# Attention features and a feed-forward layer on one core: the low bits of the converted weights move off POOL, and the scheduler's constants are new

## The chip, the cores and the metric

The kernel runs on one core of one Trainium2 chip. The metric is device time in microseconds (us) of one execution; lower is better. The result is compared with the median of the runs of the kernel before.

## The reference

Attention is computed with random positive features, and its output goes through a feed-forward layer. Inputs: q, k, v of 8 batches x 8 heads x 576 tokens x 64, omega 128 x 64, w_in 512 x 2048, w_out 2048 x 512.

```python
def phi(x):                                  # x scaled by 64 ** -0.25
    proj = np.einsum('bhsd,md->bhsm', x, omega)
    h = proj - np.sum(x * x, axis=-1, keepdims=True) / 2.0
    h = h - np.max(h, axis=-1, keepdims=True)
    return np.exp(h) / np.sqrt(m)
q_p, k_p = phi(q_s), phi(k_s)
kv = np.einsum('bhsm,bhsd->bhmd', k_p, v)
z = np.sum(k_p, axis=2)
num = np.einsum('bhsm,bhmd->bhsd', q_p, kv)
den = np.einsum('bhsm,bhm->bhs', q_p, z)[..., None] + 1e-06
x = (num / den)            # to 4608 tokens x 512
h = x @ w_in
out = np.maximum(0.01 * h, h) @ w_out
```

The two weight matrices arrive as 64-bit floating-point numbers, and the kernel reads them as pairs of 32-bit words.

## The kernel before

The 4608 tokens are cut into 9 blocks of 512. For each block a query stage computes the attention output x of 4 head pairs, and a feed-forward stage multiplies x by w_in, applies the leaky maximum and multiplies by w_out. While the feed-forward of block j runs, the attention of block j+1 is prepared. Large products are made of fp16 pieces: a 32-bit value is split into a high fp16 part and a low one (the rest), and three products of parts are summed. The helper `high` makes a high part or a scaled copy (L446/L448 on DVE or L450 on ACT), `low_` makes a low part by subtraction (L456, on POOL or DVE), and `two` adds or subtracts two tiles (L1048, on POOL or DVE). From block 3 on, the first product goes by a seven-product scheme whose mixed weights pass through a scratch in DRAM (`w1s`). The last two blocks use it for the second product too.

Before the first feed-forward stage the weights have to be made ready. `Weight.load` brings each matrix in 8 pieces of 1 MB into one of 4 `big` buffers (tiles fix_big). `Weight.convert` turns one piece of 128 x 1024 64-bit numbers into 32-bit ones in three steps: ACT scales the high words (L570), POOL takes the top three bits of the low words into a temporary (L573), and DVE shifts the former and joins the latter in (L575). PE then sums squares of the result (L582). From the largest sum (L590 on DVE, a PE broadcast at L484, five short DVE instructions) comes one power of two for the matrix, `pow_w`, and `Weight.split` makes the two fp16 parts with it (L448, L450, L456, L601).

The first query block and the first two key batches are computed in 32 bits (`Whole`): a load of qT or kT, squares on ACT (L733), products on PE (L759), a maximum and a subtraction on DVE (L766, L787), exponentials on ACT (L790, L979), the key sums on PE (L880), which are copied out as `kv` (L448/L450 to fix_kv), and the query's products with them (L1006). A division (L1016 to L1019, DVE) gives x in the tiles fix_x and fix_y. `turned_parts` splits x (L450 on ACT, L456 on POOL or DVE, tiles fix_xn) and turns it by a DMA transpose (L933, tile fix_xt). The first feed-forward products (L1374) read fix_xt.

The order of the work isn't written by hand. `Plan` collects some 3100 operations with the engines that may run each, a cost in us for each, and priorities. `Plan.order` then plays a list schedule: it takes the open operations by priority, gives each the engine that is free first by its rules (`PRICE` weighs an engine, `ONLY` forces one), and fixes each engine's order. `TURNS` shifts the priority of single operations, `HELD` delays single ones, `LATER` and `PACE` set priorities of whole stages (weights, keys, queries), and `S_GATE` says after which feed-forward operation the mixed weights may start. Each engine then runs its instructions strictly in that order, as does the queue of SP, which issues every DMA. Where the schedule leaves PE without work for 0.4 us or more, `between` lays filler matmuls that nobody reads (`busy`, L1447).

## Time and profile before

| | |
|---|---|
| median of 3 runs | 935.9 us (931.59 to 936.74) |
| the profiled execution | 934.14 us, of it the span from first to last instruction 932.4 us |
| PE busy | 901.2 us (97%), 8543 matmuls |
| DVE / ACT / POOL busy | 748.3 (80%) / 550.8 (59%) / 384.4 us (41%) |
| mean granted TensorE clock | 0.988 of full speed |
| HBM traffic over the span | 105 GB/s; all DMA 157 GB/s |

The profile shows one execution. PE is TensorE's matmuls and PEld its weight loads, DVE is VectorE, ACT is ScalarE, POOL is GpSimd, and SPq is the queue of SyncE. A busy PE counts pipelined matmuls, so 97% doesn't say that it works at its peak all the time. "idle before" a group is the time in which its engine waited for it, with the one that released it.

### The profile page before, as it was taken

The numbers are of one execution on the slowest core, as the hardware profiler recorded it, in microseconds if no ns is written. First come the engines' busy times: TensorE is split into PE (matmuls) and PEld (weight loads), VectorE is DVE, ScalarE is ACT, GpSimd is POOL, SyncE is SP. The second block draws the span as 40 slices with busy tenths as digits, with TensorE's granted clock in tenths as the row PEclk, the third lists the DMA queues.
The fourth block names the chain that finished last, engine by engine and source line by source line (L and its number), as shares of the span: only waits on it lengthen the run. The fifth ranks groups of instructions, "written<-read, shape, count | busy, mean of one in ns | idle before, by whom it ended". The sixth has DMA issues, their size and how long they took to land.

```text
span 932.4 us, 21056 instructions
## 1 busy us (share of the span) xinstructions
PE 901.2 (97%) x8543; PEld 617.5 (66%) x8543; DVE 748.3 (80%) x1355; ACT 550.8 (59%) x899; POOL 384.4 (41%) x311
## 2 busy tenths in 40 slices
PE   7789999999999998999999999989999999999997
PEld 7687555555545444588558855776568646888886
DVE  5689777799989987888888798968868885785872
ACT  5557776647634554568657686668558633552640
POOL 5957733334313542214222441214135556541550
PEclk9989999999999999999999999999999999999999
DMA  8867336963566549796886969597739962532401
GB/s 351 329 190 226 69 72 158 207 173 73 114 157 170 138 131 206 174 210 193 160 186 164 218 145 219 126 197 148 162 78 245 185 114 65 174 80 70 136 1 46
DMA packets 258769, 145.92 MB, mean 157 GB/s; under 512 B 191344, under 2 KB 238704, under 8 KB 257648
## 3 DMA queue, kind: packets, MB, share of 16 engines
q1 hardware_dynamic: 258672, 144.58, 64.0%
q8 instruction: 67, 1.10, 0.5%
q14 instruction: 30, 0.25, 0.1%
HBM read 81.36 MB, written 16.78 MB: 105 GB/s over the span
## 4 chain that ended last, share of the span: by engine, by line
PE 74%; DMA 10%; DVE 8%; POOL 5%; issue 2%; ACT 1%; SPq 1%; DVEq 0%; ACTq 0%; POOLq 0%
PE fixps_ffn L1396 24%; PE fixps_ffn L1282 16%; PE fixps_ffn L1374 10%; PE lateps_ffn L1282 5%; PE lateps_ffn L1206 5%; PE attps_pj L680 4%; POOL fix_wt L573 4%; PE fixps_ffn L1206 3%; DMA proj_t<-proj_z 2%; DMA fix_xt<-fix_xn 2%; DMA w1s<-fix_y 2%; DMA att_qp<-att_ph 1%; PE attps_mi L999 1%; DVE proj_st L687 1%; DMA fix_big<-w_in 1%
## 5 line engine op out<-in xcount | busy, mean ns | idle before, releaser
L1396 PE MATMUL fixps_ffn<-fix_wt,fix_big 128*128 128x512 f16 x1344 | 304.2, 381 | 0.0
L1396 PEld LDWEIGHTS <-fix_big 128*128 128x128 f16 x1344 | 127.2, 98 | 145.6 <-issue 2.2
L1282 PEld LDWEIGHTS <-fix_wt 128*128 128x128 f16 x2016 | 195.3, 98 | 25.9 <-issue 0.7
L1282 PE MATMUL fixps_ffn<-fix_xt,fix_wt 128*128 128x256 f16 x1572 | 182.5, 274 | 0.5 <-ACT fix_row L450 0.5
L456 POOL TENSOR_TENSOR fix_big<-fix_row,fix_big 128x512 f16<-128x512 f32 x66 | 85.3, 1293 | 154.7 <-ACT fix_big L450 124.1
L1374 PE MATMUL fixps_ffn<-fix_xt,fix_wt 128*128 128x512 f16 x576 | 129.2, 379 | 1.2 <-DMA fix_xt<-fix_xn 1.2
L1374 PEld LDWEIGHTS <-fix_wt 128*128 128x128 f16 x576 | 54.9, 98 | 64.4 <-issue 1.5
L687 DVE TENSOR_REDUCE proj_st<-attps_pj 128x8 f32<-128x1024 f32 x68 | 72.6, 1074 | 13.8 <-PE attps_pj L680 13.6
L709 ACT ACTIVATE att_p<-att_p,shift 128x1024 f32<-128x1024 f32 x52 | 59.4, 1143 | 32.5 <-DVE att_p L706 32.3
L450 ACT ACTIVATE fix_big<-fix_row 128x512 f16<-128x512 f32 x115 | 70.1, 624 | 11.8 <-DVE fix_row L1048 7.1
L573 POOL TENSOR_SCALAR fix_wt<-fix_big 128x1024 uint32<-128x1024 uint32 x16 | 65.1, 4070 | 13.5 <-DMA fix_big<-w_in 11.0
L456 DVE TENSOR_TENSOR fix_big<-fix_row,fix_big 128x512 f16<-128x512 f32 x73 | 62.6, 868 | 5.9 <-ACT fix_big L450 5.3
L706 DVE SCALAR_TENSOR_TENSOR att_p<-attps_pj,proj_sc,proj_st 128x1024 f32<-128x1024 f32 x52 | 66.2, 1276 | 0.1
L456 DVE TENSOR_TENSOR att_ph<-att_p,att_ph 128x1024 f16<-128x1024 f32 x48 | 62.2, 1296 | 4.5 <-ACT att_ph L450 4.5
L640 ACT ACTIVATE proj_z<-proj_nat 128x512 f32<-128x512 f32 (+1 forms) x56 | 36.3, 648 | 49.5 <-DMA proj_t<-proj_z 30.5
L456 POOL TENSOR_TENSOR fix_xn<-fix_x,fix_xn 128x512 f16<-128x512 f32 (+1 forms) x23 | 26.5, 1154 | 87.6 <-ACT fix_xn L450 75.9
L1305 ACT ACTIVATE fix_row<-fix_row 128x512 f32<-128x512 f32 x69 | 42.8, 624 | 19.1 <-DVE fix_row L1297 18.7
L680 PE MATMUL attps_pj<-om,proj_t 64*128 64x128 f16 x1416 | 50.5, 217 | 2.7 <-DMA proj_t<-proj_z 2.7
L450 ACT ACTIVATE att_ph<-att_p 128x1024 f16<-128x1024 f32 x49 | 51.5, 1050 | 2.1 <-PE attps_mi L894 1.6
L1282 PE MATMUL lateps_ffn<-fix_xt,fix_wt 128*128 128x256 f16 x444 | 51.4, 273 | 0.0
L680 PEld LDWEIGHTS <-proj_t 64*128 64x128 f16 x1416 | 39.7, 94 | 17.7 <-issue 10.8
L664 DVE SCALAR_TENSOR_TENSOR proj_z<-proj_nat,proj_sc,proj_z 128x512 f16<-128x512 f32 (+1 forms) x52 | 47.0, 906 | 4.1 <-ACT proj_z L450 3.9
(237 smaller groups left out, 1729.1 us busy)
## 6 DMA issues: line engine op xcount, KB each, us to landing
fix_wt<-w1s SPq DMA_DIRECT2D x38, 512.0 KB, 4.7
fix_wt<-w1s SPq DMA_DIRECT2D x38, 384.0 KB, 3.6
fix_v<-vn SPq DMA_DIRECT2D x16, 650.0 KB, 5.7
out<-fix_row SPq DMA_DIRECT2D x34, 256.0 KB, 2.3
...
```

The costliest lines, as they stand in the source:

```text
L450: ("ACT", act(n, int(pointer)), lambda: nc.scalar.activation(dst(), src(), AF.Copy, scale=1.0 if scale is None else value()), False),
L456: o = ways([(e, c, lambda g=g: g.tensor_tensor(dst(), a(), b(), op=ALU.subtract), True) for e, c, g in (("POOL", pool_(n), nc.gpsimd), ("D ...
L573: ways([("POOL", pool_(1024), lambda: nc.gpsimd.tensor_scalar(top3(), low(), 2.0 ** -29, 7.0, op0=ALU.mult, op1=ALU.min), True)], r=[b], w ...
L664: op("DVE", stt(n) + 0.15, lambda: nc.vector.scalar_tensor_tensor(zl(), heads(), up(), zh(), op0=ALU.mult, op1=ALU.subtract), port=True, r ...
L680: nc.tensor.matmul(at(pj)[:, 512 * h + c * M:512 * h + (c + 1) * M], at(self.t)[r, 2 * (c0 + c) + x, :], om[r, w, :], start=(x + w == 0), ...
L687: op("DVE", dve(n * M), lambda: nc.vector.tensor_reduce(row(0), pv(), axis=AX.X, op=ALU.max), r=[pj], w=[st], prio=prio)
L706: op("DVE", dve(n * M), lambda: nc.vector.scalar_tensor_tensor(p(), pv(), down(), row(2).rearrange("p (g o) -> p g o", o=1).broadcast_to([ ...
L709: op("ACT", act(n * M, 1), lambda: nc.scalar.activation(flat(p()), flat(p()), AF.Exp, bias=shift), w=[p32], r=["ones"], prio=prio)
L1206: nc.tensor.matmul(o, ga(gp, f, 1)[:, 0, P * t:P * t + P], w(f, wp), start=(first and place + f % 2 + t + gp + wp == 0), stop=(place == 3 ...
L1282: nc.tensor.matmul(o, unit(at(wb[c]), u)[:, wp, P * a:P * a + P], mixes[j, c][n][1](xp), start=(first and a == 0 and i == 0), stop=(a == 1 ...
L1374: nc.tensor.matmul(at(ph), wk[wp][:, c:c + P], xt[:, xp, :], start=(k + wp + xp == 0), stop=(k == KT - 1 and wp == 1))
L1396: nc.tensor.matmul(at(po), part(f, gp)[:, t * P:(t + 1) * P], wf[wp], start=(n == 0 and f % 4 == 0 and gp == wp), stop=(n == 3 and f % 4 = ...
```

## The change

One edit changes what is computed where. The top three bits of a low word are no longer made on POOL (a multiply and a minimum on 32-bit integers). They are made either on ACT, which reads the upper 16 bits of the low word, multiplies by 7.49 / 65536 and rounds to an integer, or on DVE, which shifts the low word right by 29. The scheduler picks: of the 16 pieces, 11 go to ACT (4 of w_in, 7 of w_out) and 5 to DVE (4 and 1). The ACT way rounds where the others cut off.

The other edits are numbers of the scheduler: the cost of the square sums 0.5 to 0.6, of a group of exponentials by 0.04 less, the cost of the 32-bit products, and all tables and weights.

```diff
+U16 = mybir.dt.uint16
-PACE = {'k': 20.5, 'q': 15.5, 'w1': 23, 'w1s': 0, 'w2': 8, 'w2s': 2}
+PACE = {'k': 11.5, 'q': 31.5, 'w1': 26, 'w1s': 4, 'w2': 12, 'w2s': 0}
-LATER = {'s': 40.0, 'w1': -245.0, 'w2': -440.0, 'k': -700.0, 'q': -375.0, 'm': 1860.0}
+LATER = {'s': 330.0, 'w1': -260.0, 'w2': -555.0, 'k': -190.0, 'q': -1135.0, 'm': 1985.0}
-S_GATE = 24
+S_GATE = 18
-PJ, PJ32 = 0.07, 0.5
+PJ, PJ32 = 0.07, 0.53
+LOW3 = 7.49 * 2.0 ** -16
 TURNS = {
-    4: -7005.2331, 7: -5110.3778, 15: -57900.145, 21: -5388.6643, 30: -5105.2668, 37: 5334.3764, 42: -2222.8973,
+    4: -5217.9625, 15: -29625.3333, 30: -29636.835, 64: 775.2483, 69: 5964.4575, 70: 8369.6977, 71: 2070.5909,
...
 ONLY = {
-    38: "DVE", 91: "DVE", 174: "DVE", 176: "DVE", 180: "DVE", 181: "POOL", 184: "POOL", 242: "POOL", 246: "DVE",
+    92: "ACT", 94: "POOL", 128: "DVE", 129: "DVE", 133: "DVE", 138: "DVE", 143: "DVE", 158: "DVE", 178: "POOL",
...
-    PRICE = {'PE': 1.0, 'ACT': 2.464, 'DVE': 7.416, 'POOL': 4.818, 'SP': 1.0}
+    PRICE = {'PE': 1.0, 'ACT': 2.957, 'DVE': 6.674, 'POOL': 2.341, 'SP': 1.0}
...
-            ways([("POOL", pool_(1024), lambda: nc.gpsimd.tensor_scalar(top3(), low(), 2.0 ** -29, 7.0, op0=ALU.mult,
-                   op1=ALU.min), True)], r=[b], w=[tmp], prio=prio)
+            ways([("ACT", act(1150), lambda: nc.scalar.activation(top3(), at(b).bitcast(
+                   U16).rearrange("p (a b) -> p a b", b=4)[:, :, 1], AF.Copy, scale=LOW3), False),
+                  ("DVE", 0.85, lambda: nc.vector.tensor_scalar(top3(), low(), 29, None, op0=ALU.logical_shift_right), True)],
+                 r=[b], w=[tmp], prio=prio)
...
-            op("PE", 0.5, squares, r=[f], w=[self.sums], prio=prio, slack=6.0)
+            op("PE", 0.6, squares, r=[f], w=[self.sums], prio=prio, slack=6.0)
...
-                op("ACT", n * (act(M, 2) - 0.07), powers, r=[pj, st, self.sc], w=[p32], prio=prio)
+                op("ACT", n * (act(M, 2) - 0.11), powers, r=[pj, st, self.sc], w=[p32], prio=prio)
```

The operations are the same in number, but nearly all stand elsewhere in the order of their engine. Lines of the changed file lie 5 higher up to the conversion and 7 higher behind it (L456 is L461 there, L933 is L940). Three places show the move. The names are those of tiles: fix_xn is the split x of a head pair, fix_wt a piece of a weight, fix_big a loaded piece, fix_kv the copied key sums, att_qp the query's exponentials, fix_row_92 here a piece of qT or its square.

POOL, first part of the program; before, from its fifth piece of the weights on:

```order
L837 COPY row_scale<-pow_v_130 128x1 x4
L837 COPY row_scale<-pow_v_130 64x1
L573 TENSOR_SCALAR fix_wt_73<-fix_big_88 128x1024
L573 TENSOR_SCALAR fix_wt_75<-fix_big_89 128x1024
L573 TENSOR_SCALAR fix_wt_77<-fix_big_90 128x1024
L573 TENSOR_SCALAR fix_wt_79<-fix_big_91 128x1024
L456 TENSOR_TENSOR fix_xn_86<-fix_x_84,fix_xn_86 128x512
L456 TENSOR_TENSOR fix_wt_67<-fix_wt_68,fix_wt_67 128x1024
```

and now, from its first computing instruction on:

```order
L844 COPY row_scale<-pow_v_130 128x1 x4
L844 COPY row_scale<-pow_v_130 64x1
L461 ISA
L461 TENSOR_TENSOR fix_xn_86<-fix_x_84,fix_xn_86 128x512
L461 TENSOR_TENSOR fix_wt_67<-fix_wt_68,fix_wt_67 128x1024
L461 TENSOR_TENSOR fix_wt_65<-fix_wt_66,fix_wt_65 128x1024
L461 TENSOR_TENSOR fix_xn_87<-fix_y_85,fix_xn_87 128x512
```

The low part of the first head pair's x stood behind 8 conversions on POOL and stands behind none.

SP's queue around the first transpose; before:

```order
L558 DMA fix_big_90<-w_out 128x2x1024
L732 DMA proj_nat_177<-kT 128x512
L558 DMA fix_big_91<-w_out 128x2x1024
L933 DMA_TRANSPOSE fix_xt_99<-fix_xn_86 128x8x128
L732 DMA fix_row_92<-qT 128x512
L732 DMA proj_nat_178<-kT 128x512
```

and now:

```order
L563 DMA fix_big_90<-w_out 128x2x1024
L940 DMA_TRANSPOSE fix_xt_99<-fix_xn_86 128x8x128
L563 DMA fix_big_91<-w_out 128x2x1024
L739 DMA proj_nat_177<-kT 128x512
L739 DMA fix_row_92<-qT 128x512
L739 DMA proj_nat_178<-kT 128x512
```

The load of qT for the fourth head pair stands behind that transpose in both.

DVE where the second pair of key sums is copied out; before:

```order
L446 CAST fix_wt_67<-fix_wt_68 128x1024
L456 TENSOR_TENSOR fix_wt_65<-fix_wt_66,fix_wt_65 128x1024
L601 SCALAR_TENSOR_TENSOR fix_wt_80<-fix_wt_64,pow_w_132,fix_wt_80 128x1024
L448 TENSOR_SCALAR fix_kv_81<-attps_mi_173,pow_v_130 128x4x64
L1016 TENSOR_SCALAR att_r_165<-fixps_ffn_115 128x4
L1017 RECIPROCAL att_r_165<-att_r_165 128x4
L766 TENSOR_REDUCE proj_st_189<-attps_pj_171 128x8
```

and now ACT, which has taken the copy:

```order
L455 ACTIVATE fix_wt_66<-fix_wt_66,pow_w_132 128x1024
L740 ACTIVATE proj_z_180<-proj_nat_178 128x512
L455 ACTIVATE fix_kv_81<-attps_mi_173,pow_v_130 128x4x64
L455 ACTIVATE fix_wt_65<-fix_wt_66 128x1024
L455 ACTIVATE fix_kv_81<-attps_mi_173 128x4
L986 ACTIVATE att_qp_163<-fixps_ffn_115,shift 128x512
```

The copy stood behind two parts of w_in on DVE, and stands behind one scaled copy of w_in and a square on ACT.

Counted over the program: POOL's two-input instructions (L456 and L1048 before) go from 243 to 291, those of DVE on the same lines from 259 to 210. DVE gets 22 more casts, 4 more copies and 9 more scaled copies (L446 and L448), besides its 5 shifts. The filler matmuls go from 113 to 70, those ahead of the first L1374 from 104 to 57. PE's other matmuls are the same in number, ahead of the first L1374 and behind it.

## Rows read from the trace of the kernel before

**Rows 1.** Stretches: PE, PEld, DVE, ACT, POOL busy (instructions), granted clock, DMA share, GB/s

```profile
25.00:50.00 25.00, 20.66 (x227) 18.35 (x229) 17.35 (x29) 12.42 (x17) 24.54 (x11) 0.86 0.89 323
50.00:75.00 25.00, 22.10 (x233) 21.05 (x232) 21.93 (x34) 16.87 (x22) 14.02 (x6) 0.86 0.45 133
90.00:150.00 60.00, 59.41 (x484) 32.73 (x484) 45.95 (x89) 45.25 (x81) 35.21 (x26) 1.00 0.36 84
150.00:350.00 200.00, 198.31 (x1618) 102.62 (x1617) 177.25 (x329) 107.26 (x178) 76.20 (x64) 1.00 0.64 150
350.00:600.00 250.00, 246.37 (x2621) 164.83 (x2620) 215.48 (x433) 167.26 (x275) 75.40 (x80) 0.99 0.82 179
```

**Rows 2.** Waits of PE from 95 us on: us in total, times, longest

```profile
PE attps_mi L1001 <- DMA att_qp<-att_ph: 3.2, 2, 3.0
PE attps_pj L680 <- DMA proj_t<-proj_z: 2.7, 5, 1.6
PE attps_mi L999 <- DVE fix_y L1019: 2.6, 1, 2.6
```

**Rows 3.** The chain that ended last, 48 to 92 us: start, us, what

```profile
47.86 2.20 POOL fix_xn L456
...
51.48 5.51 DMA fix_row<-qT
...
60.31 3.12 DVE fix_wt L456
63.43 3.06 DVE fix_wt L601
66.49 0.40 DVE fix_kv L448
...
67.17 2.02 DVE proj_st L766 x2
...
83.30 6.87 DMA fix_xt<-fix_xn
...
90.21 1.89 PE fixps_ffn L1374 x8
```

**Rows 4.** Timeline of POOL, 8 to 50 us: start, us, idle before

```profile
30.70 17.08 POOL L573 TENSOR_SCALAR fix_wt<-fix_big 128x1024 uint32<-128x1024 uint32 x4
```

**Rows 5.** Instructions on tile fix_wt, 10 to 125 us: ns min/median/max, first and last start

```profile
L573 POOL TENSOR_SCALAR fix_wt<-fix_big x16: 3679/3724/4752, 11.5 to 111.6; 128x1024 uint32<-128x1024 uint32 x16
L575 DVE SCALAR_TENSOR_TENSOR fix_wt<-fix_wt,fix_wt x16: 1214/1223/1225, 16.5 to 115.7; 128x1024 uint32<-128x1024 uint32 x16
L456 DVE TENSOR_TENSOR fix_wt<-fix_wt,fix_wt x3: 1212/1218/3115, 60.3 to 90.1; 128x1024 f16<-128x1024 f32 x3
L601 DVE SCALAR_TENSOR_TENSOR fix_wt<-fix_wt,pow_w,fix_wt x3: 1562/2178/3141, 63.4 to 91.2; 128x1024 f16<-128x1024 f32 x3
L448 DVE TENSOR_SCALAR fix_wt<-fix_wt,pow_w x2: 744/746/747, 57.9 to 58.6; 128x1024 f32<-128x1024 f32 x1, 128x1024 f16<-128x1024 f32 x1
L456 POOL TENSOR_TENSOR fix_wt<-fix_wt,fix_wt x2: 2137/2314/2492, 60.2 to 62.9; 128x1024 f16<-128x1024 f32 x2
```

**Rows 6.** Timeline of SP's queue at the first transpose

```profile
50.08 1.34 SPq L933 DMA_TRANSPOSE fix_xt<-fix_xn  x1
```

**Rows 7.** Timeline of DVE and ACT around the first head pair's x

```profile
37.61 1.16 ACT L570 ACTIVATE fix_wt<-fix_big 128x1024 f32<-128x1024 f32 x1 [1.35 <-DMA fix_big<-w_in]
39.25 1.22 DVE L575 SCALAR_TENSOR_TENSOR fix_wt<-fix_wt,fix_wt 128x1024 uint32<-128x1024 uint32 x1 [3.60 <-POOL fix_wt L573]
41.72 0.63 ACT L450 ACTIVATE fix_xn<-fix_x 128x512 f16<-128x512 f32 x1 [2.95 <-DVE fix_x L1019]
```

**Rows 8.** Waits of PE over the span: us in total, times, longest

```profile
PE fixps_ffn L1006 <- ACT fix_kv L450: 2.9, 1, 2.9
```

**Rows 9.** Groups by line: instructions, busy us, mean ns, idle before

```profile
L456 POOL TENSOR_TENSOR fix_big<-fix_row,fix_big 128x512 f16<-128x512 f32 x66 | 85.3, 1293 | 154.7 <-ACT fix_big L450 124.1 <-DVE fix_big L446 26.5 <-DMA proj_nat<-kn 3.8
L573 POOL TENSOR_SCALAR fix_wt<-fix_big 128x1024 uint32<-128x1024 uint32 x16 | 65.1, 4070 | 13.5 <-DMA fix_big<-w_in 11.0 <-DVE fix_wt L575 1.3
L456 DVE TENSOR_TENSOR fix_big<-fix_row,fix_big 128x512 f16<-128x512 f32 x73 | 62.6, 868 | 5.9 <-ACT fix_big L450 5.3
```

More of the change, by code (lines that the diff above doesn't have):

```diff
@@ L66 @@
 TURNS = {
[48 rows of a table removed]
[46 rows of a table added]
 }
 HELD = {
[6 rows of a table removed]
[6 rows of a table added]
 }
 ONLY = {
-    38: "DVE", 91: "DVE", 174: "DVE", 176: "DVE", 180: "DVE", 181: "POOL", 184: "POOL", 242: "POOL", 246: "DVE",
-    247: "POOL", 250: "DVE", 261: "DVE", 270: "DVE", 275: "DVE", 279: "POOL", 298: "DVE", 302: "DVE", 303: "DVE",
-    306: "DVE", 307: "POOL", 347: "DVE", 361: "POOL", 362: "DVE", 363: "DVE", 369: "DVE", 375: "DVE", 381: "DVE",
-    382: "DVE", 386: "DVE", 387: "DVE", 389: "DVE", 394: "DVE", 396: "DVE", 399: "DVE", 402: "DVE", 406: "DVE",
-    425: "DVE", 432: "DVE", 433: "DVE", 439: "POOL", 443: "DVE", 444: "DVE", 452: "POOL", 457: "DVE", 467: "DVE",
@@ L130 @@
-    505: "POOL", 546: "DVE", 579: "DVE", 580: "POOL", 598: "POOL", 605: "POOL", 615: "DVE", 628: "DVE", 636: "POOL",
-    644: "DVE", 651: "DVE", 660: "POOL", 663: "DVE", 667: "DVE", 672: "DVE", 680: "POOL", 704: "DVE", 734: "POOL",
-    740: "POOL", 754: "DVE", 755: "POOL", 761: "POOL", 778: "POOL", 802: "DVE", 834: "POOL", 840: "DVE", 849: "POOL",
-    863: "DVE", 871: "DVE", 881: "DVE", 882: "DVE", 888: "DVE", 906: "DVE", 907: "DVE", 912: "POOL", 919: "DVE",
-    920: "DVE", 932: "POOL", 936: "POOL", 952: "DVE", 959: "DVE", 960: "POOL", 971: "DVE", 972: "DVE", 1009: "DVE",
@@ L135 @@
-    1043: "DVE", 1057: "DVE", 1058: "POOL", 1092: "DVE", 1117: "DVE", 1133: "POOL", 1141: "DVE", 1163: "DVE",
-    1190: "DVE", 1209: "DVE", 1215: "DVE", 1235: "DVE", 1245: "DVE", 1259: "DVE", 1299: "DVE", 1302: "DVE",
-    1303: "DVE", 1324: "DVE", 1347: "DVE", 1348: "POOL", 1349: "DVE", 1350: "DVE", 1357: "DVE", 1442: "DVE",
-    1450: "DVE", 1566: "DVE", 1591: "DVE", 1598: "DVE", 1634: "DVE", 1671: "DVE", 1890: "POOL", 1927: "POOL",
-    1932: "DVE", 1956: "DVE", 1995: "DVE", 2046: "DVE", 2268: "DVE", 2380: "DVE", 2601: "DVE", 2622: "POOL",
@@ L140 @@
-    2630: "DVE", 2633: "DVE", 2698: "DVE", 2733: "POOL", 2895: "DVE",
+    92: "ACT", 94: "POOL", 128: "DVE", 129: "DVE", 133: "DVE", 138: "DVE", 143: "DVE", 158: "DVE", 178: "POOL",
+    181: "POOL", 189: "POOL", 192: "POOL", 212: "DVE", 222: "ACT", 248: "DVE", 252: "DVE", 261: "DVE", 265: "ACT",
+    266: "DVE", 278: "DVE", 286: "DVE", 311: "DVE", 314: "DVE", 322: "DVE", 368: "DVE", 371: "DVE", 376: "DVE",
+    389: "DVE", 390: "DVE", 394: "DVE", 406: "DVE", 424: "DVE", 427: "DVE", 431: "DVE", 432: "DVE", 436: "DVE",
@@ new lines @@
+    437: "DVE", 448: "DVE", 449: "DVE", 450: "DVE", 452: "DVE", 455: "DVE", 456: "DVE", 464: "DVE", 467: "DVE",
+    504: "DVE", 505: "POOL", 529: "ACT", 580: "POOL", 596: "DVE", 597: "DVE", 605: "POOL", 614: "ACT", 615: "DVE",
+    620: "DVE", 627: "DVE", 631: "DVE", 632: "DVE", 635: "DVE", 639: "DVE", 644: "DVE", 655: "DVE", 659: "DVE",
+    663: "DVE", 667: "DVE", 676: "DVE", 680: "DVE", 686: "DVE", 714: "DVE", 716: "POOL", 717: "DVE", 733: "DVE",
+    739: "DVE", 746: "DVE", 761: "POOL", 802: "DVE", 827: "DVE", 848: "DVE", 855: "POOL", 872: "POOL", 882: "DVE",
@@ new lines @@
+    888: "DVE", 907: "DVE", 911: "DVE", 919: "DVE", 920: "DVE", 923: "DVE", 927: "DVE", 935: "DVE", 936: "DVE",
+    939: "DVE", 940: "DVE", 944: "DVE", 952: "DVE", 956: "DVE", 996: "DVE", 1006: "DVE", 1007: "DVE", 1010: "DVE",
+    1011: "POOL", 1017: "DVE", 1025: "DVE", 1040: "DVE", 1057: "DVE", 1090: "DVE", 1109: "DVE", 1149: "DVE",
+    1150: "POOL", 1163: "DVE", 1171: "DVE", 1182: "DVE", 1192: "DVE", 1202: "DVE", 1207: "DVE", 1212: "DVE",
+    1235: "DVE", 1238: "DVE", 1302: "DVE", 1307: "DVE", 1330: "DVE", 1346: "DVE", 1351: "POOL", 1371: "DVE",
@@ new lines @@
+    1469: "DVE", 1667: "DVE", 1671: "DVE", 1690: "DVE", 1780: "POOL", 1940: "DVE", 1941: "DVE", 2002: "DVE",
+    2003: "DVE", 2068: "POOL", 2150: "DVE", 2263: "DVE", 2271: "DVE", 2281: "DVE", 2301: "DVE", 2310: "DVE",
+    2311: "DVE", 2330: "DVE", 2339: "DVE", 2345: "DVE", 2359: "DVE", 2363: "DVE", 2374: "DVE", 2505: "DVE",
+    2528: "DVE", 2577: "DVE", 2608: "DVE", 2633: "POOL", 2640: "ACT", 2647: "DVE", 2657: "DVE", 2660: "DVE",
+    2670: "DVE", 2679: "DVE", 2682: "DVE", 2692: "DVE", 2696: "DVE", 2718: "DVE", 2731: "POOL", 2732: "ACT",
@@ L141 @@
+    2736: "POOL", 2754: "POOL", 2805: "DVE", 2810: "POOL", 2818: "DVE", 2865: "DVE", 2911: "DVE", 2965: "DVE",
+    2966: "POOL", 2971: "DVE", 2973: "DVE", 3019: "DVE", 3083: "DVE", 3095: "ACT",
 }
```

104 rows, old and new, of tables (HELD, TURNS) are left out of this document.

## The prediction

> **What bounds the kernel now.** I read the stretches first. From 90 us on PE is busy nearly all the time: 198.3 of 200 us in 150 to 350 and 246.4 of 250 in 350 to 600 [rows 1]. Its waits from 95 us on are short; the three longest groups come to 3.2 + 2.7 + 2.6 = 8.5 us [rows 2]. So the end of the program is the moment at which dense feed-forward work can start, plus a stream of PE work that the change leaves the same in number, plus those few waits. The moment is 90.21 us, where the chain of waits has the first long run of L1374 [rows 3]. What decides is the stretch ahead of it.
>
> In that stretch the chain begins with POOL. In 25 to 50 us POOL is busy 24.54 of 25 us, PE 20.7, DVE 17.4, ACT 12.4 [rows 1], and what it does are the low bits of the weights: the second four of w_in run from 30.70 for 17.08 us [rows 4], at 3.7 to 4.75 us each [rows 5]. Then the chain goes as follows [rows 3]: at 47.86 POOL makes the low part of the first head pair's x (2.20 us); SP's queue stands at the transpose of that x until 50.08 [rows 6]; the load of qT for the fourth head pair, which is behind it, starts at 51.48 and takes 5.51 us; DVE is held up by two parts of w_in of 3.12 and 3.06 us, behind which the copy of the key sums stands (66.49); then come the maxima at 67.17, x and its transpose at 83.30 (6.87 us), and 90.21. The reader should see a chain that passes through four engines and is late from its first link.
>
> **The change part by part.** *Low bits leave POOL.* POOL had done the cast's other half long before it could have: the cast on ACT starts at 41.72 and takes 0.63 us [rows 7], POOL begins at 47.86 [rows 3]. The difference, 47.86 - 42.35 = 5.5 us, goes, as no conversion is ahead of it any more. The cast itself may come earlier too. It waited 2.95 us for DVE, and DVE had lost 3.60 us waiting for POOL's low bits [rows 7]. But three of the new ACT conversions now stand ahead of the cast. I price them like L570, 1.16 us [rows 7], together 3.5 us. ACT was free at 41.72 - 2.95 = 38.8; one L570 moves behind the cast (-1.16), and the 1.35 us that it waited for its load [rows 7] go with it: 38.8 - 2.5 + 3.5 = 39.8, at best 1.9 us earlier than 41.72. So the first transpose, and with it the load of qT, comes 5.5 to 7.4 us earlier; I take the middle, 6.5.
>
> *DVE up to the maxima.* Of the two parts of w_in ahead of the maxima (3.12 + 3.06 = 6.2 us) one L601 stays, at 1.56 us when nothing disturbs it [rows 5]; the subtraction goes to POOL. The copy of the key sums goes to ACT, behind one scaled copy. New on DVE are four shifts. No row has such an instruction. The nearest are a scaled copy of 128 x 1024 on DVE, 0.745 us, and the joining step on the same words, 1.22 us [rows 5]; as the shift reads one tensor, I take 0.75 and keep the other end, so 3.0 to 4.9 us. Net 6.2 - 1.6 - 3.0 = 1.6 us gained, at the other end 0.3 lost; I take 0.7.
>
> *The clock.* In 50 to 75 us the granted clock is 0.86 of full speed [rows 1]: some 7 us at 1.2 GHz and the rest at 2.4, so that PE's work there took up to 3.5 us longer. It fell after PE had waited 2.9 us for the copied key sums [rows 8]. If these waits shrink, 0 to 3.5 us come back; I take 1.0.
>
> Sum for the start: 6.5 + 0.7 + 1.0 = 8.2 us. The upper end is 7.4 + 1.6 + 3.5 = 12.5. The lower end comes from DVE. In 50 to 75 it is busy 21.93 of 25 us [rows 1], and if it can't do earlier what fills that stretch, no more than its free 3.1 us can be won.
>
> *The conversions of w_out.* Seven go to ACT, 7 x 1.16 = 8.1 us, one to DVE. They run between 65 and 115 us, before and beside the first feed-forward block. About half fall after 90, where ACT is busy 45.25 of 60 us [rows 1]; with 4 us more it is at 82%, so I cost them at nothing. The cover is ACT's free time; if it is gone at the wrong place, an L570 late by one or two places costs up to 2 us. POOL, which is rid of 65.1 us [rows 9], takes more low parts of the first block instead.
>
> *The new order behind it.* The 48 more two-input instructions on POOL cost 1293 ns each against 868 on DVE [rows 9], so POOL's total stays (48 x 1.29 = 62 us for 65.1), and DVE loses 49 x 0.87 = 42.5 us and gains 35 casts and copies of at most 0.75 (26 us) and 5 shifts (3.7): 12 us less, spread over the program. PE's waits of 8.5 us [rows 2] hang on places that are all laid anew; nothing says in which direction, so 0, with both ends at 6 us. The 43 filler matmuls that go stood where PE had no work, so they count nothing.
>
> **Sum.** 934.1 - 8.2 = 925.9, so 926 us. This is against the profiled execution of 934.14 us (932.4 of span and 1.7 around it), which is 1.8 us below the median of the runs shown and within their spread.
>
> **A rule against it.** POOL's kind of work changes. Beside L573 no DVE joining step ever took more than 1.225 us, while L573 itself went from 3.68 to 4.75 [rows 5]: there POOL was the one that waited. Beside POOL's two subtractions of the same kind, which start at 60.2 and 62.9, a DVE subtraction took 3.115 instead of 1.212 us [rows 3, 5]. The Trainium skill, "SBUF — State Buffer", Who interferes with whom, says that a VectorE instruction with two SBUF inputs and a GpSimd one that reads SBUF exclude each other, and that the one to start first holds the port for its whole length. The trace agrees, with 1.07 us on the one side and 1.90 on the other. By that rule 48 more such instructions on POOL can each hold up DVE, which my sum doesn't count; the second rival does.
>
> **The rivals.** *First: the start is held by DVE and the loads anyway.* For it: DVE's 88% in 50 to 75, and ACT's wait of 1.35 us for the last piece of w_in at 37.61 [rows 7], which the change can't speed up. Against it: DVE had 7.6 free us in 25 to 50 [rows 1] and waited for POOL in them. Then 3.1 us are won: 931. Chance 0.17.
>
> *Second, slower: POOL's subtractions block DVE in the middle.* Place: 150 to 600 us, where DVE is busy 177.3 + 215.5 = 392.7 of 450 us [rows 1]. Price: 48 x 1.90 = 91 us if each meets a DVE instruction, less the 12 that DVE is relieved of, is 79, of which 450 of 840 us get 42. DVE would then be at 435 of 450. It decides from about 428 (95%), since DVE's gaps lie where it waits for PE and can't be moved. With half of the 42 reaching PE, 925.9 + 21 = 947. Against it: POOL was busy just as long before, and 868 ns on DVE already holds such meetings. Chance 0.10.
>
> *Third: more is won.* The start gives its upper end, 12.5 us, and PE's waits lose 6 with a relieved DVE: 915.6. Chance 0.10.
>
> *Fourth: the change doesn't take the work off the path.* ACT reads 16-bit numbers 8 bytes apart. If that costs twice an L570, three conversions more by 3.5 us stand ahead of the cast: 934.1 - 8.2 + 3.5 = 929.4. Chance 0.03.
>
> **How the numbers follow.** My forecast has 0.60; with the bounds of the start and of the waits its own range is 919 to 933. The range is 914 to 938: it takes in the first, third and fourth rival and leaves out the second and the tails, less than 2 in 10. About 0.5% is what a measurement of this kernel can tell from no change, so faster means below 931.2 and slower above 940.6. Faster gets 0.52 of my 0.60, 0.08 of the first rival, 0.10 of the third and 0.03 of the fourth, 0.73. The second is slower, 0.10. The rest, 0.17, is the same.
>
> **What would show it.** In the profile of the changed kernel: the first low part of x on POOL should start near 41 us instead of 47.86, the first transpose near 43 instead of 50.08, qT's load near 45 instead of 51.48; the transpose of the fourth head pair near 75 instead of 83.30; the long run of L1374 near 82 instead of 90.21. The new ACT conversion should take about 1.16 us, the DVE shift 0.75. PE's waits from 95 us on should stay near 8.5 us in their three longest groups, and DVE below 95% in 150 to 600. I am wrong if the long run of L1374 starts later than 87, or if it starts early and the gain is gone by the end.

## The result, and the profile after

The changed kernel takes **923.4 us** (median of 4 runs, 919.42 to 926.38), the kernel before 935.5 us beside it (931.59 to 936.74). The ratio is 0.9875, 95% interval 0.9827 to 0.9923: 1.25% faster. The profiled execution has a span of 921.0 us, against 932.4.

I read it in the order of the prediction. First the stretches (columns as in [rows 1]):

```profile
25.00:50.00 25.00, 22.88 (x286) 20.71 (x287) 21.66 (x33) 18.99 (x23) 1.69 (x1) 1.00 1.04 385
50.00:75.00 25.00, 24.08 (x249) 21.13 (x249) 23.41 (x39) 23.30 (x32) 11.45 (x7) 1.00 0.77 198
90.00:150.00 60.00, 55.85 (x479) 32.68 (x475) 47.48 (x97) 39.49 (x79) 21.98 (x24) 0.94 0.58 123
150.00:350.00 200.00, 198.37 (x1568) 101.31 (x1569) 179.72 (x313) 98.11 (x162) 87.58 (x76) 0.98 0.59 140
350.00:600.00 250.00, 248.91 (x2667) 168.68 (x2666) 221.41 (x433) 170.20 (x279) 95.84 (x102) 1.00 0.79 181
```

In 25 to 50 us POOL falls from 24.54 to 1.69 us, and the clock of the first two stretches is 1.00 instead of 0.86. But 90 to 150, where PE had been full, now has 55.85 of 60 us and a clock of 0.94. The start got better and a later place worse.

The chain that ended last (start, us, what; compare [rows 3]):

```profile
23.80 10.15 DMA fix_big<-w_in
33.98 1.15 ACT fix_wt L575
...
53.30 2.01 PE attps_pj L766 x32
...
55.33 1.23 DVE proj_st L773
...
69.99 5.75 DMA fix_xt<-fix_xn
75.78 2.10 PE fixps_ffn L1381 x9
```

POOL's low bits are gone from it, and so are the two steps of 3.12 and 3.06 us on DVE. The last transpose goes at 69.99 instead of 83.30, and the long run of feed-forward work starts at 75.78 instead of 90.21 [rows 3]: **14.4 us earlier**, where the end comes only 11.4 us earlier. So 3.0 us net are lost behind the start. (In a second trace of the changed kernel, the run `changed_again` below, the long run starts at 77.17 and the span is 923.6 us: 13.0 and 8.8 us earlier, 4.2 us lost.)

The first link, in the timelines of POOL, of SP's queue and of ACT, whose square (L740) waits for the load of qT to land:

```profile
37.28 1.69 POOL L461 TENSOR_TENSOR fix_xn<-fix_x,fix_xn 128x512 f16<-128x512 f32 x1 [19.59 <-ACT fix_xn L455]
```

```profile
38.99 3.08 SPq L940 DMA_TRANSPOSE fix_xt<-fix_xn  x1
...
43.26 0.42 SPq L739 DMA_DIRECT2D fix_row<-qT  x1
```

```profile
50.49 0.63 ACT L740 ACTIVATE fix_row<-fix_row 128x512 f32<-128x512 f32 x1 [1.12 <-DMA fix_row<-qT]
```

The low part starts 10.6 us earlier, and the load of qT is issued 8.2 us earlier (51.48 in [rows 3]). But it lands only 6.6 us earlier: the square starts at 50.49 instead of 57.07. Instructions on tile fix_wt, in 0 to 130 us, give the prices (columns as in [rows 5]):

```profile
L582 DVE SCALAR_TENSOR_TENSOR fix_wt<-fix_wt,fix_wt x16: 1196/1226/1875, 20.8 to 92.5; 128x1024 uint32<-128x1024 uint32 x16
L578 ACT ACTIVATE fix_wt<-fix_big x11: 1117/1149/1182, 26.0 to 91.1; 128x1024 uint32<-128x1024 uint16 x11
L580 DVE TENSOR_SCALAR fix_wt<-fix_big x5: 683/686/689, 18.8 to 75.1; 128x1024 uint32<-128x1024 uint32 x5
```

And the waits of PE from 85 us on (total, times, longest), the three longest groups:

```profile
PE attps_pj L687 <- DMA proj_t<-proj_z: 5.5, 5, 2.2
PE attps_mi L489 <- ACT fix_kv L455: 1.9, 1, 1.9
PE fixps_ffn L1289 <- ACT fix_row L455: 1.0, 1, 1.0
```

They come to 8.4 us, as before (8.5 in [rows 2]), but they are other waits. Two of 1.9 and 2.2 us now lie in 110 to 150 us, where the kernel before had none over 0.4; its two longest, of 2.6 us at 356 and 3.0 us at 613, are gone.

### The profile page after: what moved, and what is told of

Read it like the earlier page. It is cut to its first block, busy times and chain, and to the rows that moved or that the text cites. A ratio compares the mean times of both kernels' runs of the same rounds, so it can differ in the third digit from the quotient of the medians.

```text
span 921.0 us, 20971 instructions
## 1 busy us (share of the span) xinstructions
PE 894.9 (97%) x8500; PEld 609.4 (66%) x8500; DVE 766.5 (83%) x1344; ACT 535.8 (58%) x877; POOL 381.2 (41%) x344
## 4 chain that ended last, share of the span: by engine, by line
PE 66%; DVE 17%; DMA 8%; ACT 4%; issue 2%; SPq 2%; DVEq 0%; ACTq 0%
PE fixps_ffn L1403 23%; PE fixps_ffn L1289 13%; PE fixps_ffn L1381 8%; PE lateps_ffn L1289 5%; PE lateps_ffn L1213 5%; PE attps_pj L687 4%; PE fixps_ffn L1213 3%; DMA proj_t<-proj_z 3%; DVE att_ph L461 2%; DVE proj_st L694 2%; DVE att_p L713 1%; DVE proj_st L699 1%; DMA fix_xt<-fix_xn 1%; DVE proj_z L671 1%; SPq L1069 1%
## 5 line engine op out<-in xcount | busy, mean ns | idle before, releaser
L1289 PE MATMUL fixps_ffn<-fix_xt,fix_wt 128*128 128x256 f16 x1608 | 185.9, 273 | 1.3 <-ACT fix_row L455 1.0
L461 POOL TENSOR_TENSOR fix_big<-fix_row,fix_big 128x512 f16<-128x512 f32 x97 | 127.2, 1317 | 137.9 <-ACT fix_big L455 95.5
L1381 PE MATMUL fixps_ffn<-fix_xt,fix_wt 128*128 128x512 f16 x576 | 131.2, 383 | 1.1 <-DMA fix_xt<-fix_xn 1.1
L1381 PEld LDWEIGHTS <-fix_wt 128*128 128x128 f16 x576 | 55.2, 99 | 64.8 <-issue 3.7
L461 DVE TENSOR_TENSOR att_ph<-att_p,att_ph 128x1024 f16<-128x1024 f32 x51 | 69.2, 1359 | 5.6 <-ACT att_ph L455 5.4
L455 ACT ACTIVATE fix_big<-fix_row 128x512 f16<-128x512 f32 x106 | 64.7, 624 | 6.0 <-DVE fix_row L1055 3.1
L461 POOL TENSOR_TENSOR fix_xn<-fix_x,fix_xn 128x512 f16<-128x512 f32 (+1 forms) x24 | 26.2, 1092 | 74.3 <-ACT fix_xn L455 74.3
L649 DVE TENSOR_REDUCE proj_sq<-proj_z 128x8 f32<-128x512 f32 (+1 forms) x56 | 39.6, 709 | 20.4 <-ACT proj_z L647 20.2
L671 DVE SCALAR_TENSOR_TENSOR proj_z<-proj_nat,proj_sc,proj_z 128x512 f16<-128x512 f32 (+1 forms) x52 | 51.8, 999 | 0.9 <-ACT proj_z L455 0.7
L1304 DVE TENSOR_TENSOR fix_row<-fix_row,fixps_ffn 128x512 f32<-128x512 f32 x56 | 38.0, 681 | 12.2 <-PE fixps_ffn L1289 7.9
L1289 PE MATMUL lateps_ffn<-fix_xt,fix_wt 128*128 128x256 f16 x408 | 47.2, 273 | 0.0
L1386 ACT ACTIVATE fix_row<-fixps_ffn 128x512 f32<-128x512 f32 x48 | 28.6, 596 | 29.7 <-PE fixps_ffn L1381 29.7
```

The lines of the kernel that those rows point to most:

```text
L455: ("ACT", act(n, int(pointer)), lambda: nc.scalar.activation(dst(), src(), AF.Copy, scale=1.0 if scale is None else value()), False),
L461: o = ways([(e, c, lambda g=g: g.tensor_tensor(dst(), a(), b(), op=ALU.subtract), True) for e, c, g in (("POOL", pool_(n), nc.gpsimd), ("D ...
L671: op("DVE", stt(n) + 0.15, lambda: nc.vector.scalar_tensor_tensor(zl(), heads(), up(), zh(), op0=ALU.mult, op1=ALU.subtract), port=True, r ...
L1289: nc.tensor.matmul(o, unit(at(wb[c]), u)[:, wp, P * a:P * a + P], mixes[j, c][n][1](xp), start=(first and a == 0 and i == 0), stop=(a == 1 ...
L1381: nc.tensor.matmul(at(ph), wk[wp][:, c:c + P], xt[:, xp, :], start=(k + wp + xp == 0), stop=(k == KT - 1 and wp == 1))
```

## The experiments

Three questions: does the gain come from the engine of the low bits or from the rebuilt order; if from both, what in the order; and where do the 3 us go? In kernels with added or removed lines the same code has another line number (L942 and L939 are L940, L741 is L739, L1383 and L1380 are L1381, L458 is L461 or L456, L610 is L608 or L601, L591 is L589 or L582, L572 is L575 or L570; L584 is the joining step, L582 on ACT the low bits).

### The swap and the order, taken apart

**Old order, new operations.** Only the function that the POOL entry calls is another:

```diff
+            def low_bits():
+                if (self.name, i) in (("w1", 0), ("w1", 1), ("w1", 2), ("w1", 5), ("w2", 3)):
+                    nc.vector.tensor_scalar(top3(), low(), 29, None, op0=ALU.logical_shift_right)
+                else:
+                    nc.scalar.activation(top3(), at(b).bitcast(U16).rearrange("p (a b) -> p a b", b=4)[:, :, 1], AF.Copy, scale=LOW3)
-            ways([("POOL", pool_(1024), lambda: nc.gpsimd.tensor_scalar(top3(), low(), 2.0 ** -29, 7.0, op0=ALU.mult,
-                   op1=ALU.min), True)], r=[b], w=[tmp], prio=prio)
+            ways([("POOL", pool_(1024), low_bits, True)], r=[b], w=[tmp], prio=prio)
```

> The order of the kernel before, instruction for instruction, with the planner still counting the low bits on POOL; only the engine that makes them is another: DVE for pieces 0, 1, 2, 5 of w_in and 3 of w_out, ACT for the other eleven, as in the changed kernel. Theory A (the gain is the start, and it comes from POOL's low bits leaving the chain): POOL's first low part of x starts near 42 us instead of 47.86, the first transpose near 43 to 45 instead of 50.08, the first long run of feed-forward work near 80 to 83 instead of 90.21, and the time is 924 to 928 us. Rival B (the gain comes from the rebuilt tables and constants, the engine of the low bits matters little): the long run stays within 2 us of 90 and the time is 931 to 937 us. In between, the share of the 12 us that this kernel gains is the share of the swap.

Measured: 930.6 us, ratio 0.996 (0.9945 to 0.9974). Rival B's number; theory A's first link came, and then most of it was lost. POOL, SP's queue and the chain:

```profile
38.83 1.16 POOL L458 TENSOR_TENSOR fix_xn<-fix_x,fix_xn 128x512 f16<-128x512 f32 x1 [14.40 <-ACT fix_xn L452]
```

```profile
40.37 4.76 SPq L942 DMA_TRANSPOSE fix_xt<-fix_xn  x1
45.19 0.57 SPq L741 DMA_DIRECT2D fix_row<-qT  x1
```

```profile
55.24 3.04 DVE fix_wt L458
58.29 3.06 DVE fix_wt L610
...
80.88 5.90 DMA fix_xt<-fix_xn
86.82 3.40 PE fixps_ffn L1383 x15
```

The low part starts 9.0 us earlier, but the transpose behind it holds SP's queue for 4.76 us (1.34 in [rows 6]), so the load of qT is issued 6.3 us earlier; its square on ACT starts at 50.65, 6.4 us earlier. The two long steps on DVE still stand ahead of the maxima, the last transpose is 2.4 us earlier and the long run 3.4. The time is 3.5 us shorter than that of the kernel before on the same chip (934.2).

**New order, old operations.** Both entries of the changed kernel call POOL:

```diff
+            low_bits = lambda: nc.gpsimd.tensor_scalar(top3(), low(), 2.0 ** -29, 7.0, op0=ALU.mult, op1=ALU.min)
+            ways([("ACT", act(1150), low_bits, False), ("DVE", 0.85, low_bits, True)],
```

> The order of the changed kernel, instruction for instruction, but every low-bit operation is done by POOL as before, at the place in the order where ACT or DVE has it now. Theory A: POOL's queue again has 8 conversions of 3.7 to 4.75 us ahead of or around the first low part of x, the big buffers come free late and the loads of w_in with them; the first transpose comes at 48 us or later instead of 38.99, the long run at 88 us or later instead of 75.78, and the time is 933 to 945 us. Rival B: the new order carries the gain by itself: the long run before 80 us and 922 to 928 us.

Measured: 953.2 us, ratio 1.0206 (1.0186 to 1.0225), worse than either theory had it. POOL's timeline shows why:

```profile
17.84 32.56 POOL L578 TENSOR_SCALAR fix_wt<-fix_big 128x1024 uint32<-128x1024 uint32 x7
50.47 2.20 POOL L461 TENSOR_TENSOR fix_xn<-fix_x,fix_xn 128x512 f16<-128x512 f32 x1
```

Seven conversions in a row stand ahead of the first low part of x. Rival B falls: the new order with POOL's low bits loses 19 us to the kernel before, with the new operations it wins 10 to 12. Both mixed kernels keep an order that the scheduler made for the other operations. What it would make of the new tables if it knew the low bits on POOL, or of the old tables if it knew the new operations, was not run.

**The new order with w_in alone on POOL** (the same edit, under `if self.name == "w1"`).

> The order of the changed kernel with POOL making the low bits of w_in alone; those of w_out stay with ACT and DVE. Theory A (w_in's conversions on POOL stand ahead of the first low part of x): POOL again runs seven conversions in a row from 17.8 to about 50.4 us, the first transpose is issued near 52.7 instead of 38.99, as with all sixteen on POOL (953.2 us); what is better than that run is what the eight of w_out, between 52 and 110 us, hold up: 4 to 10 us, so 943 to 949. Rival G2 (the eight of w_out do most of the harm): 930 to 938.

Measured: 938.7 us, ratio 1.0065 (1.0035 to 1.0095), between the two expectations. The first link is as theory A had it (seven conversions from 18.51 to 51.1 us), and PE's timeline has the long run 16.1 us later than in the changed kernel:

```profile
91.90 2.10 PE L1383 MATMUL fixps_ffn<-fix_xt,fix_wt 128*128 128x512 f16 x9 [1.00 <-DMA fix_xt<-fix_xn]
```

So in this order the conversions of w_in on POOL cost 938.7 - 923.4 = 15.3 us and those of w_out 953.2 - 938.7 = 14.6 us.

**The old order with w_in alone on the new engines** (w_out stays on POOL).

> The old order with the new operations for w_in alone; the eight conversions of w_out stay on POOL. Theory A (only w_in counts; those of w_out cost nothing and give nothing on either engine): 930 to 932 us, as with all sixteen moved (930.6), long run within 1 us of 86.82. Rival G (POOL's conversions of w_out between 62 and 85 us hold up the last low part of x, or DVE's steps on the same words, so that part of the 3.5 us is theirs): 932 to 934 us, long run after 88.

Measured: 930.4 us, ratio 0.9954 (0.9935 to 0.9974), long run at 85.95; theory A. In the old order those of w_out give nothing.

### What in the old order holds the start

**The four DVE steps of w_in later.** To the old order with the new operations:

```diff
     order = plan.order()
     fill = between(order)
+    block = [o for n in (178, 175, 186, 189, 196, 197, 215, 201, 198) for o in order if o.number == n]
+    order = [o for o in order if o not in block]
+    place = 1 + next(n for n, o in enumerate(order) if o.number == 112)
+    order[place:place] = block
```

The numbers are the planner's own: 178, 175, 186 and 189 are the four steps, 196, 197, 201 and 198 conversions of w_out, 215 a load of w_out, 112 the transpose of the third head pair's x.

> The old order with the new operations (930.6 us, long run from 86.82), and in it the four steps on DVE that make low parts of w_in (they ran at 55.24, 58.21, 65.59 and 66.77, together 8.6 us, ahead of the maxima and of the low parts of x) moved behind the low parts of x of the second and third head pair, together with the first conversion of w_out, whose buffers they free. Theory A2 (the swap frees the first link by 5.6 us, and the old order loses most of that again on DVE, which stands in those four steps; the rest of the gain of the changed kernel is this): the maxima start near 56 instead of 61.94, the transposes near 63 instead of 71.18, the long run at 78 to 81, and the time is 922 to 925 us. Rival F (what holds the old order is elsewhere: SP's queue, the two places for x's parts, the loads of w_in): the long run stays after 85 and the time is 928 to 932.

Measured: 931.9 us, ratio 0.997 (0.995 to 0.9991). Theory A2 falls in this form: SP issues the two transposes at 67.75 instead of 71.18, 3.4 us earlier, but the last one still at 80.26. On ACT the cast of the last head pair's x starts at 78.38, as late as before the move (78.78). And that transpose no longer decides: PE reaches its long run at 86.95 without a wait for it. In PE's row ahead of that run stand the square sums of the first piece of w_out (L591), which now wait 1.75 us for DVE's joining step; behind this wait and one of 1.46 us the granted clock falls to 0.50, and it is 0.77 in 75 to 90 us (1.00 before the move).

**The same in the kernel before** (old operations).

> The kernel before, POOL making all low bits, with the same four steps on DVE moved behind the low parts of x. If the two hindrances add up (theory A2 with independent parts): the maxima come 6 to 8 us earlier, the long run at 82 to 85 instead of 90.21, 927 to 930 us. If POOL's conversions hold this order whatever DVE does (the two only help together): the long run at 88 to 90, 932 to 935 us.

Measured: 938.3 us, ratio 1.0047 (1.0021 to 1.0073): not additive; it is slower. The last transpose goes at 87.73, when POOL has made the low part (86.55, 1.15 us) behind three conversions in a row (73.25 to 86.47). PE's long run at 92.59 doesn't wait for it either; PE had waited 3.45 us for the joining step ahead of the square sums, with a clock of 0.66 in 75 to 90 us.

**The four steps behind the last products of x** (`127` in place of `112` in the edit).

> As the run with the parts of w_in later (931.9 us, where the moved steps came ahead of the last head pair's x instead of ahead of the second's and third's, and the last transpose stayed at 80.26 us), but moved one step further, behind the last products of x for the fourth head pair. Theory A3 (in the old order DVE's row of steps up to the last transpose sets the start, and what of w_in and w_out stands in it delays it one for one): the last transpose goes at 73 to 76 us, the long run starts at 78 to 82 instead of 86.8, 922 to 926 us. Rival F2 (DVE isn't it: ACT's scaled copies, the loads or the transposes hold the last head pair at the same place): the last transpose stays within 2 us of 80, 929 to 932.

Measured: 932.2 us, ratio 0.9993 (0.9969 to 1.0017). Theory A3 falls, F2 holds: DVE had the last products ready at 73.7 us, and ACT made the cast at 79.51 only. ACT's timeline just ahead of it:

```profile
74.89 1.13 ACT L582 ACTIVATE fix_wt<-fix_big 128x1024 uint32<-128x1024 uint16 x1 [0.75 <-DVE fix_wt L458]
76.08 1.13 ACT L572 ACTIVATE fix_wt<-fix_big 128x1024 f32<-128x1024 f32 x1
77.28 1.13 ACT L582 ACTIVATE fix_wt<-fix_big 128x1024 uint32<-128x1024 uint16 x1
78.46 1.14 ACT L572 ACTIVATE fix_wt<-fix_big 128x1024 f32<-128x1024 f32 x1
79.51 0.61 ACT L452 ACTIVATE fix_xn<-fix_y 128x512 f16<-128x512 f32 x1
```

The low bits of w_out (L582), once on POOL's queue, now stand on ACT's with the other conversions (L572), ahead of that cast. But here too PE's own row comes last. The square sums wait for the joining step, which ends at 79.5 behind the four moved steps, and PE goes on at a clock of 0.50 in 78.5 to 88.7 us:

```profile
79.57 1.03 PE L591 MATMUL fixps_ffn<-fix_wt 128*128 128x128 bf16 x8 [5.67 <-DVE proj_sc L657]
...
91.75 4.05 PE L1383 MATMUL fixps_ffn<-fix_xt,fix_wt 128*128 128x512 f16 x18
```

The long run at 91.75 waits for no transpose.

**The last head pair's whole x ahead of the weights** (the block is now `128, 129, 130, 178, 175, 186, 189, 196, 197, 215, 201, 202, 198, 206`, put behind `127`; 128 to 130 are that x's cast, low part and transpose, 202 and 206 two more conversions of w_out).

> The old order with the new operations, and in it the whole chain of the last head pair's x (the cast on ACT, the low part on POOL, the transpose) put directly behind its products, ahead of the four steps of w_in on DVE and of the first conversions of w_out on ACT, which stood ahead of the cast there (in the three runs of this order ACT made that cast at 78.4 to 79.5 us, behind six conversions, though its data was there at 73.7). Theory A4 (after the swap the old order is held by conversions of weights that stand ahead of x on ACT and DVE both, and moving one of the two alone, as the earlier two runs did, shows nothing): the last transpose goes at 73 to 77 us instead of 80 to 81.4, the long run starts at 79 to 83, 923 to 928 us. Rival F3 (the features of the next batch on DVE and PE, which the moved steps delay, or PE's own wait for the parts of w_in, take back what x gains): the last transpose is early but the long run stays after 85, 929 to 933.

Measured: 934.8 us, ratio 1.0004 (0.9986 to 1.0021). Rival F3. SP's queue, PE, and DVE:

```profile
65.93 7.38 SPq L942 DMA_TRANSPOSE fix_xt<-fix_xn  x3
```

```profile
76.65 1.04 PE L591 MATMUL fixps_ffn<-fix_wt 128*128 128x128 bf16 x8 [6.57 <-DVE proj_sc L657]
...
88.47 2.76 PE L1383 MATMUL fixps_ffn<-fix_xt,fix_wt 128*128 128x512 f16 x6
```

```profile
70.94 3.38 DVE L610 SCALAR_TENSOR_TENSOR fix_wt<-fix_wt,pow_w,fix_wt 128x1024 f16<-128x1024 f32 x2
74.24 1.21 DVE L458 TENSOR_TENSOR fix_wt<-fix_wt,fix_wt 128x1024 f16<-128x1024 f32 x1
75.38 1.21 DVE L584 SCALAR_TENSOR_TENSOR fix_wt<-fix_wt,fix_wt 128x1024 uint32<-128x1024 uint32 x1
```

All three transposes are through the queue by 73.3 us; in the three other runs of this order with all sixteen on the new engines the last one was issued at 80.3 to 81.4. But in PE's row the square sums of the first piece of w_out and the key sums of the next batch stand ahead of the long run; the first now wait 6.57 us for DVE's joining step (L584, which ends at 76.6), and behind that wait PE runs at a granted clock of 0.50 in 75 to 90 us, so that the key sums take longer too.

**The same in the kernel before.**

> The kernel before with the same rows moved, POOL making all low bits. Theory A4: the last low part of x no longer stands behind conversions on POOL either, but the first link does (47.86 us, first transpose near 50): the long run starts at 85 to 88 instead of 90.21, 929 to 932 us. If the first link is all that counts: 90 and 933 to 935.

Measured: 942.9 us, ratio 1.01 (1.0069 to 1.0131). Neither number: worse, with a wait of 7.92 us ahead of the square sums.

What follows from the five: in the old order several rows of work end within a few microseconds of each other (w_in's steps on DVE, w_out's conversions on ACT, x's transposes, w_out's squares on PE). Moving one brings the next: each of the five moves made PE wait 1.75 to 7.92 us ahead of w_out's square sums, with a stretch at half clock behind it. No kernel with x and those squares both early was run. Which of the rebuilt order's moves carry the other 11.0 us of the earlier start was not isolated; that stays open.

### Where 3 us are given back

In the changed kernel SP's timeline and PE's read, at 115 to 147 us:

```profile
135.83 6.80 SPq L1069 DMA_DIRECT2D w1s<-fix_wt  x10
142.73 1.35 SPq L673 DMA_TRANSPOSE proj_t<-proj_z  x1
```

```profile
115.17 0.49 PE L489 MATMUL attps_mi<-ident,mx_v 128*128 128x128 f32 x2 [1.92 <-ACT fix_kv L455]
146.19 1.68 PE L687 MATMUL attps_pj<-om,proj_t 64*128 64x128 f16 x30 [2.24 <-DMA proj_t<-proj_z]
```

and the granted clock (the 1.00, 0.50, ... of the columns in [rows 1]) right behind the two waits and after them:

```profile
115.60:119.00 3.40, 3.40 (x10) 1.22 (x8) 3.07 (x7) 1.15 (x3) 1.61 (x2) 0.50 0.12 29
146.40:156.50 10.10, 10.10 (x61) 7.11 (x56) 6.56 (x13) 4.47 (x9) 3.14 (x4) 0.50 0.98 197
156.60:160.00 3.40, 3.40 (x17) 1.53 (x16) 3.18 (x8) 1.68 (x3) 0.00 (x0) 1.00 0.45 87
```

The transposed load at 142.73 is of data that DVE had ready at 130.3. It stands behind writes of scaled weights (24 of about 0.5 us each, at 128.9 to 152.0 us, 19 of them ahead of the load), which the rebuilt order puts there; in the kernel before they were issued at 152.8 to 176.2.

The two waits and half of the two stretches at half clock come to 1.92 + 2.24 + 1.7 + 5.1 = 10.9 us, far more than 3. The rest was won back later, where the kernel before has two such places and the changed one has neither (from 157 us on its clock stays at 1.00 and no wait of PE is over 1.4 us). The kernel before:

```profile
356.44 0.19 PE L999 MATMUL attps_mi<-fix_kv,att_qp 128*128 128x65 f16 x1 [2.63 <-DVE fix_y L1019]
612.82 0.20 PE L1001 MATMUL attps_mi<-fix_kv,att_qp 128*128 128x65 f16 x1 [3.01 <-DMA att_qp<-att_ph]
```

```profile
357.10:360.50 3.40, 3.40 (x10) 1.22 (x9) 2.81 (x10) 2.06 (x4) 0.90 (x1) 0.50 0.58 164
613.10:616.50 3.40, 3.40 (x23) 2.40 (x20) 2.98 (x9) 0.47 (x1) 0.00 (x0) 0.50 0.99 345
```

They cost it 2.63 + 3.01 + 1.7 + 1.7 = 9.0 us. So 3.0 is the balance of a loss of 10.9 us and a gain of 9.0, and of smaller waits.

**The transposed load ahead of 12 writes** (12 in SP's timeline, and one other transposed load; the expectation says 15):

```diff
     fill = between(order)
+    def behind(number, other):
+        o, = (o for o in order if o.number == number)
+        order.remove(o)
+        order.insert(1 + next(n for n, x in enumerate(order) if x.number == other), o)
+    behind(727, 600)
```

> The changed kernel with one instruction moved: the transposed load that SP's queue issues at 142.73 us, of data that DVE had ready at 130.3, goes ahead of 15 of the writes of scaled weights that stood before it, to the first place at which its destination is free. Theory C (3 us of the 14.4 won at the start are given back in 110 to 157 us, by waits that SP's queue and the order make, and by the half clock after them): PE's wait of 2.2 us at 144 goes, the 10.2 us at half clock from 146.3 on go with it (5.1 us of work lost), and the time falls by 4 to 7.3 us, to 916 to 919. Rival D (the wait goes but the half clock is not its doing and comes anyway): 2.2 us at most, 921 to 923. Rival E (PE would have waited later anyway, for DVE): the same time as the changed kernel within 0.2%.

**And the product of the maxima behind one more feed-forward run** (also `behind(711, 308)`).

> As the run before (the transposed load ahead of 15 writes), and on PE the small product that broadcasts the maxima of the next batch, for which PE waits 1.92 us at 113 to 115 us, goes behind the next run of 12 feed-forward products. Theory C: that wait goes too, and the 3.4 us at half clock from 115.6 on (1.7 us of work), so 2 to 3.6 us less than the run before: 913 to 916. Rival D: 1.9 us at most less than the run before. Rival E: no difference to the run before; the chain behind the maxima then ends 2.6 us later and PE waits for it further on.

**The changed kernel again**, as the measure of both.

> The changed kernel itself once more, unaltered, for an interval beside the runs of this study: 921.5 to 924.5 us. The kernel with the transposed load ahead (920.0) and that with the maxima too (918.6) are then compared with it.

Measured: 920.0 us, 918.6 us and 923.4 us; ratios 0.9856 (0.9835 to 0.9877), 0.9838 (0.9819 to 0.9857) and 0.9872 (0.984 to 0.9904). The first lies between the numbers of theories C and D, the second above all that was expected of it by theory C (913 to 916), the third as expected. The intervals overlap, so by time alone I can't tell them apart; the traces can. With the transposed load ahead:

```profile
133.06 1.44 SPq L673 DMA_TRANSPOSE proj_t<-proj_z  x1
```

```profile
143.37 1.01 PE L687 MATMUL attps_pj<-om,proj_t 64*128 64x128 f16 x30
```

```profile
110.00:160.00 50.00, 47.12 (x396) 26.08 (x395) 44.25 (x102) 30.58 (x58) 18.55 (x21) 1.00 0.68 155
```

The wait is gone, the stretch has a clock of 1.00 instead of 0.86, and SP issues the first writes of the output at 168.97 us instead of 174.10 (167.56 with the maxima moved too). That is theory C's mechanism with 5.1 of its 7.3 us there; 4.0 us are left at the end (a span of 917.0 us). Rival D is excluded for the second wait: its half clock was there in both traces of the changed kernel and in neither with the load ahead. For the first wait the half clock is no sure follower: in the second trace of the changed kernel PE waits 1.82 us at the same place, with the load ahead 1.93 us, and both times the clock stays at 1.00. Moving the maxima took that wait away, and PE waited 1.33 us for the next step of the same chain instead (rival E in part):

```profile
117.80 0.23 PE L1006 MATMUL attps_mi<-fix_kv,att_qp 128*64 128x65 f16 x2 [1.33 <-DVE fix_kv L915]
```

The kernel with both, 918.6 us, has the lowest median of all and is faster than the kernel before for certain; that it is faster than the changed kernel is likely, not shown.

## Why the prediction was right, and where its sum was wrong

Direction and range held, and the forecast was 2.6 us off, but that it came so close is partly luck. Two errors met in the number: the start gained 14.4 us, 6.2 more than the sum and 1.9 more than its upper end of 12.5, and 3.0 us were given back where the sum had 0.

- **What bounds the kernel**: right. A start that is 14.4 us earlier, less what is lost behind it, is the result.
- **Low bits leave POOL, 6.5 us (5.5 to 7.4)**: the load of qT landed 6.6 us earlier, in the old order 6.4, so the swap alone gives this term. Its parts were off and cancelled: the low part starts 10.6 us earlier, but the transpose then holds SP's queue for 3.08 us instead of 1.34, and the load takes 7.2 us instead of 5.5. What failed is "at best 1.9 us earlier" for the cast: it starts at 36.56 instead of 41.72 [rows 7]. I had put three conversions ahead of it and kept DVE's products where they were. But DVE had stood 3.60 us waiting for POOL [rows 7], and without that wait its products were done at 35.9 instead of 41.7.
- **DVE up to the maxima, 0.7 us**: the term that was mis-sized most. The maxima of the fourth head pair's query (the first of the two at 67.17 in [rows 3]) start at 55.33, 11.8 us earlier; 6.6 of these come with the load, so this term measured some 5.3. The two steps of 6.2 us did leave the chain, and nothing took their place at the price I had set against them; the shifts run earlier, in time that DVE had free, and DVE even waits 0.79 us for PE ahead of the maxima. With the operations alone the steps stayed (3.04 and 3.06 us). The last 2.6 of the 14.4 us came behind the maxima, where the sum had the clock's 1.0 at most.
- **The prices** held: the ACT conversion 1.149 us (1.16 predicted), the shift 0.686 (0.75). The fourth rival falls.
- **The clock, 1.0 of 3.5 us**: both half-clock stretches of the start are gone. What that alone gave was not measured.
- **w_out at nothing**: true in the old order (930.4 against 930.6). In the new order its conversions on POOL cost 14.6 us: the price of a step belongs to an order.
- **The new order behind it, 0 with ends at 6**: 3.0 us lost, inside the ends, but as the balance of 10.9 us lost and 9.0 won at the places shown above. That PE's waits still come to 8.4 us says nothing: they are other waits, and their half clock costs as much as they do. I had read them as something without a direction; the order had it, on the side of the loss in 24 writes that stand 24 us earlier among the transposed loads of SP's queue. What in the order removed the two waits at 356 and 613 us was not looked for.
- **DVE 12 us less busy**: it is 18 us busier (766.5 for 748.3). I added up all its instructions in both traces, each at the duration that its form has undisturbed (the 15th percentile): some 739 us before, 729 after, 10 less, about as predicted (the traces have 33 more casts and copies and not 35). What came on top are instructions that took over 0.25 us longer than that: some 89 of them and 71 us before, 131 and 103 us after. So the **second rival's** mechanism is there, with 32 us where I had 91 as the most. It cost no time that shows: DVE is at 401 of 450 us in 150 to 600, below the 428 that I set, and PE stood still for 2.7 us there instead of 5.3.
- **The rule against it**: the traces bear it out for POOL's subtractions. In the changed kernel 88 DVE instructions (of 0.35 us or more) with both inputs in SBUF began while POOL ran a two-input instruction, and 82 of them took longer by what POOL still had to do, less 0.13 us, to within 0.1 us: 57 us in all. Of 51 that began ahead of POOL's one took over 0.25 us longer, of 148 beside an idle POOL none, and of 88 with one input in PSUM, begun behind POOL's, none. The Trainium skill's rule in "SBUF — State Buffer", Who interferes with whom, that two SBUF inputs contend and that the order of start decides, agrees with this. For the conversions on POOL "the trace agrees" was too strong: in the kernel before, four such DVE instructions that began in the first 0.9 us of a conversion took 0.29 to 0.96 us longer, but ten that began 1.2 us or more after its start, with up to 2.5 us of it still to run, took no longer at all. There the hold doesn't last for the whole instruction.
- **The first rival, 931 us**, is what the swap alone gives: 930.6 us with a long run 3.4 us earlier, where I had 3.1. The forecast and this rival differ by the order, and the prediction had counted the rebuilt order as changing nothing but what it read in single rows. Of the third rival (the start's upper end, and PE's waits gone) the first half came true and more.

The four corners say it in one view: old order 934.2 us with the old operations and 930.6 with the new ones; new order 953.2 and 923.4. The swap is worth 3.5 us in the one and 30 in the other. Neither part is the cause alone.
